# Attention with a 128-key window and a mixture of experts on one core: folding the two score blocks of a query block into one 128-wide tile, splitting the turned weights on GpSimd, and ordering TensorE's work by tiling

## The chip, the cores and the metric

The kernel runs on one core of a Trainium2 chip. The metric is device time in microseconds of one launch; before the change the median of three runs is 1196.53 us (1192.06 to 1199.35). Engines are named as in the profile: PE is TensorE (PEld its weight loads), DVE is VectorE, ACT is ScalarE, POOL is GpSimd, SP is SyncE.

## The reference

Shapes: 8 batches, 8 heads, 576 positions, 64 per head; then 4608 tokens of 512 features, 8 experts of 512 x 1024 x 512. All float32.

```python
scores = scale * np.matmul(q, k.transpose(0, 1, 3, 2))
rel = pos[:, None] - pos[None, :]
bias = slopes[:, None, None] * (-np.abs(rel))[None]
mask = (rel >= 0) & (rel < 128)
scores = np.where(mask, scores + bias[None], -1e9)
attn = softmax(scores); x = attn @ v            # then tokens x features
logits = x @ w_gate + log1p(exp(x @ w_noise)) * noise
# two largest experts of each token, softmax over the two
out[mask] += top2_w * (relu(x[mask] @ w1[e]) @ w2[e])
```

A query sees itself and the 127 keys before it: 128 keys in all. They lie in two neighbouring blocks of 128.

## The kernel before, in words

**Stages.** The attention runs over 32 head pairs (8 batches x 4). Five query blocks of a pair (four of 128 rows and a last one of 64, in which both heads share a tile) are taken in three units: blocks (0, 1), blocks (2, 3), block (4). A unit (L534) does the following.

- `scores` (L444; L454, and L447 for block 4): q times k for the block's own 128 keys and the 128 before them, so 256 columns (128 for block 0, 192 for block 4). Head 0 uses rows 0 to 63 of the array and writes bank 0, head 1 rows 64 to 127 and bank 1. There is only this one pair of score banks: the next unit's scores follow the reading of these.
- `top` (L466, L472, DVE): one instruction for each block and head adds the bias and the mask, writes `p` and keeps the extreme, over all 256 columns.
- `soft` (L475, L479, ACT): exp over the same columns, in place, with its sum.
- `trans` (L485, L491, PE): transposes `p` in pieces of 128 columns: two for each head of a block (one for block 0, two for block 4), so 6, 8 and 2 for the three units.
- `evac` (L494; copies are L244 on ACT, L248 on DVE): copies the turned weights from PSUM to `pT`, a copy for each block.
- `weigh` (L504, L522, PE): `pT` times the values, head 0 into columns 0 to 63 of the array and head 1 into columns 64 to 127. For block 4 two of the four products use the lower 64 rows only.

After four pairs the batch's result is normalized and turned to token rows (L631), its gate computed (L654, L665) and the routing done (L700 on): a chain of small DVE instructions that ends in a list of tokens for each expert, scattered by POOL (L842).

The first wave of the mixture computes 256 tokens of each of experts 0 to 3 in float32 (L1085, L1139); its products are strewn between the attention of the later batches and the start of the second wave. The second wave (from about 400 us on) takes all 8 experts in 20 blocks of 320 to 512 tokens, in float16 split into a high and a low part. A block has 8 steps. A step is a first product of 12 matmuls (`mm1` L1082, L1088: four chunks of three) into one bank; then ACT makes the high part (`relu`, L1110), DVE the low part from bank and high part (L1129), and the second product of 12 matmuls (L1143, or L1148 flipped) takes both. Three banks serve the first products in turn: 0, 1 (the former score banks) and 5.

**What sets the order.** A planner in the kernel (class `Order`) plays all strands of work forward with a cost and a rank for each piece and issues the instructions in the order it finds; the engines run that order as written. Constants such as `STAGE`, `LATE` and `FFN1` shift ranks. Where a buffer is used again, the tile framework adds the semaphore waits.

```python
bank = [psum.tile([128, 512], F32, name=f"bank{i}") for i in range(8)]
sb, tb, ob, yb = Ring([bank[0:2]]), Ring([*bank[2:4], bank[7]]), Ring([bank[4], bank[6]]), Ring([])
```

Of the kernel before, what the change touches and what calls it, by code (L numbers as in the profile page):

```python
# [37 lines left out]
ZERO = 8.2  # L38
LOAD = 43.5
VALUES = -12.4  # L40
GATE = (-41.8, -83.8)
ROUTE = 0
SCATTER = (10.0, -1028.0, -66.0)
FFN0, FFN1 = 100.4, 316.8
WEIGHTS = -48.4
TOKENS = 70.2
STAGE = (5.1, 1.9, 12.7, -7.9, -6.3, 14.0, -6.0, -21.8)
MIDDLE = 73.7
RESULT = -61.8
WEIGHTS_LATE = 82.3  # L50
SIZES = (40.0, 1000 - 52.0)
EARLY = 1
SOON = 49.9
TIGHT = (1, 5, 7)
LATE = (-2.2, 37.9, 22.2, 61.2, 4.9, 37.3, -6.2, -4.7, 1.9, 24.7, 19.5, 35.7)
LAG = 0.2
SP_COST = 0.55
# [18 lines left out]
class Op:  # L76


    def __init__(self, on, emit, join=True):
        self.on, self.emit, self.join, self.taken = on, emit, join, False  # L80
# [9 lines left out]
class Order:  # L90
# [3 lines left out]
    def __init__(self):  # L94
        self.heap, self.seq, self.now, self.dma = [], 0, 0.0, 0.0
        self.busy = {e: 0.0 for e in ("PE", "ACT", "DVE", "POOL", "SP")}
        self.queue = {e: [] for e in self.busy}
        self.alive = 0
        self.work = {}

# [49 lines left out]
    def dispatch(self, e):  # L150
        if self.busy[e] > self.now:
            return
        while self.queue[e]:
            _, _, us, what, strand = heapq.heappop(self.queue[e])
# [3 lines left out]
            what.emit(e) if len(what.on) > 1 else what.emit()  # L158
            end = self.products(us) if e == "PE" else self.now + us
# [6 lines left out]
            return  # L166

# [37 lines left out]
def attention_moe(ctx: ExitStack, tc: tile.TileContext, qk_, v, w_gate, w_noise, noise, w1, w2,  # L205
# [7 lines left out]
    bank = [psum.tile([128, 512], F32, name=f"bank{i}") for i in range(8)]  # L213
# [11 lines left out]
    def pe(us, rank, emit, join=True):  # L225
        return Op((("PE", us, rank),), emit, join)
# [30 lines left out]
    pr = ring(ap_, 3, [128, 2, 2, 256], F32, "p")  # L257
    nmr = ring(ap_, 3, [128, 2, 2], F32, "nm")
    ptr = ring(ap_, 3, [128, 2, 4, 128], F32, "pT")
# [17 lines left out]
    relc, m1 = scratch[0][:, 0:256], scratch[0][:, 256:512]  # L277
    relc4, m14 = scratch[1][:, 0:192], scratch[1][:, 192:384]
    ident = const.tile([128, 128], F32, name="ident")
    bias = const.tile([128, H, 256], F32, name="bias")  # L280
    bias4 = const.tile([128, NP, 192], F32, name="bias4")
# [28 lines left out]
    def slope(h):  # L310
        return -8.0 * 2.0 ** -(h + 1)

    def masks():
        def mask(rel, m):
            nc.vector.tensor_scalar(m, rel, 0.0, None, op0=OP.is_lt)
            nc.vector.scalar_tensor_tensor(m, rel, float(W), m, op0=OP.is_ge, op1=OP.add)
            nc.vector.scalar_tensor_tensor(rel, m, 2.0 ** 40, rel, op0=OP.mult, op1=OP.add)

        def bias_of(e, h):
            copy(e, bias[:, h, :], relc, scale=slope(h))  # L320
# [3 lines left out]
        yield dve(0.14, -40, lambda: nc.vector.tensor_scalar(ident, relc[:, 0:128], 128.0, None, op0=OP.is_equal))  # L324
        yield dve(0.14, -40, lambda: nc.vector.tensor_scalar(before, relc[:, 0:128], 128.0, None, op0=OP.is_lt))
        yield dve(1.1, -40, lambda: mask(relc, m1))
        yield dve(0.95, -40, lambda: mask(relc4, m14))
# [83 lines left out]
    def all_values():  # L411
        for y in range(2 * B):
# [3 lines left out]
            yield from move(5e5, rank - 3, lambda: nc.sync.dma_start(  # L416
                t[:, 0:4], dram(v, b * S * DM + c, [[DM, 128], [128 * DM, 4], [1, 256]])))
            yield from move(1.3e5, rank - 3, lambda: nc.sync.dma_start(
                t[:, 4], dram(v, (b * S + S - 128) * DM + c, [[DM, 128], [1, 256]])))
# [46 lines left out]
    def top(k, blocks, s, p, nm):  # L466
        g = k % NP
        for z, i in enumerate(blocks):
            c, o = width(i), place_of(blocks, z)
            for h in range(heads(i)):  # L470
                bv = bias4[:, g] if i == 4 else bias[:, 2 * g + h, 256 - c:256]
# [10 lines left out]
    def pieces(i):  # L482
        return 4 if 0 < i < 4 else 2
# [1004 lines left out]
```

## Time and profile before

| what | before |
|---|---|
| median of 3 runs | 1196.53 us (1192.06 to 1199.35) |
| span of the profiled execution | 1193.9 us, 2.6 us below that median |
| PE busy / instructions | 1146.1 us / 7164 |
| DVE, ACT, POOL busy | 712.7, 518.4, 223.9 us |
| attention's transposes (L491) | 512 |
| last scores of the attention start | 310 us |
| first product of the second wave | 402.6 us |

The span runs from the first to the last instruction of one execution; the time of a run also has what lies around it. In the groups of instructions a line reads: source line, engine, operation, output and inputs by the program's names, shape, count, then busy time and the mean of one in ns. Matmuls are pipelined, so the duration of one (379 ns for 512 columns) is longer than the distance to the next. The windows give the busy time of each engine in a stretch; the chain of waits follows the end of the program back from releaser to releaser; the timeline lists instructions by their start.

### The profile page before, as it was taken

How to read it: one execution, taken by the hardware profiler on the slowest of the kernel's cores; microseconds unless marked ns; L12 is line 12 of the kernel's file. 1: busy time of each engine (PE TensorE's matmuls, PEld its weight loads, DVE VectorE, ACT ScalarE, POOL GpSimd, SP SyncE). 2: the span in 40 equal slices, each digit the busy share in tenths (PEclk: the TensorE clock that was granted, in tenths of full speed). 3: DMA queues.
4: the chain of work that ended last, by engine and by line, in shares of the span. 5: the costliest groups of instructions: out<-in, count | busy, mean ns of one | idle time of the engine just before them, and what ended most of it. 6: DMA issues, size and time to landing. Idle time of an engine off the chain costs nothing.

```text
span 1193.9 us, 20221 instructions
## 1 busy us (share of the span) xinstructions
PE 1146.1 (96%) x7164; PEld 666.6 (56%) x7164; DVE 712.7 (60%) x2422; ACT 518.4 (43%) x1317; POOL 223.9 (19%) x280
## 2 busy tenths in 40 slices
PE   7999999999998999999999999999999999999995
PEld 5666666666665545545445445445645654575552
DVE  7898867787866846646646746733843573372310
ACT  7777766676423514424324334422523442262311
POOL 1000100010023113203303312322303320232211
PEclk9999999999999999999999999999999999999998
DMA  9897454553277736627618617632843481342221
GB/s 325 293 327 252 145 154 156 157 167 96 83 197 216 245 120 149 184 83 195 184 38 208 173 48 192 168 64 54 239 132 63 93 261 36 62 117 45 36 27 23
DMA packets 133623, 173.32 MB, mean 145 GB/s; under 512 B 25488, under 2 KB 85136, under 8 KB 133520
## 3 DMA queue, kind: packets, MB, share of 16 engines
q1 hardware_dynamic: 115600, 131.68, 34.7%
q0 software_dynamic: 17920, 40.33, 17.6%
q8 instruction: 57, 0.93, 0.3%
q14 instruction: 46, 0.38, 0.1%
HBM read 130.57 MB, written 41.40 MB: 144 GB/s over the span
## 4 chain that ended last, share of the span: by engine, by line
PE 79%; DVE 7%; DMA 7%; issue 4%; ACT 1%; POOL 1%; SPq 0%; POOLq 0%; another core or an unknown queue 0%; DVEq 0%; ACTq 0%
PE bank L1088 24%; PE bank L1143 17%; PE bank L1148 7%; PE bank L522 5%; PE bank L491 5%; DMA mraw<-in_w_dram 5%; PE bank L454 5%; PE bank L1085 4%; PE bank L1139 4%; PE bank L1068 2%; DVE wam L989 2%; PE bank L631 2%; PE bank L654 1%; DVE p L472 1%; PE bank L447 1%
## 5 line engine op out<-in xcount | busy, mean ns | idle before, releaser
L1129 DVE SCALAR_TENSOR_TENSOR bhl<-bank,bhh 128x512 f16<-128x512 f32 (+3 forms) x160 | 97.3, 608 | 302.0 <-ACT bhh L1110 295.7
L1110 ACT ACTIVATE bhh<-bank 128x512 f16<-128x512 f32 (+3 forms) x150 | 80.5, 537 | 361.5 <-PE bank L1088 358.1
L1088 PE MATMUL bank<-bxh,w1hb 128*128 128x512 f16 (+3 forms) x640 | 222.2, 347 | 0.0
L1088 PE MATMUL bank<-bxl,w1hb 128*128 128x512 f16 (+3 forms) x640 | 222.1, 347 | 0.0
L1088 PE MATMUL bank<-bxh,w1lb 128*128 128x512 f16 (+3 forms) x640 | 222.1, 347 | 0.0
L1222 POOL DMA_INDIRECT out_dram<-yo,ix x72 | 113.2, 1572 | 562.4 <-ACT yo L244 484.7
L1088 PEld LDWEIGHTS <-w1hb 128*128 128x128 f16 x1280 | 124.4, 98 | 106.1 <-issue 2.2
L1143 PE MATMUL bank<-w2hb,bhl 128*128 128x512 f16 (+1 forms) x376 | 142.6, 379 | 6.9 <-DVE bhl L1129 6.9
L1143 PE MATMUL bank<-w2hb,bhh 128*128 128x512 f16 (+1 forms) x376 | 142.8, 380 | 0.5 <-ACT bhh L1110 0.5
L1143 PE MATMUL bank<-w2lb,bhh 128*128 128x512 f16 (+1 forms) x376 | 142.5, 379 | 0.0
L479 ACT ACTIVATE p<-p,nm 128x256 f32<-128x256 f32 (+2 forms) x288 | 133.7, 469 | 10.7 <-DVE nm L472 10.6
L1143 PEld LDWEIGHTS <-bhh 128*128 128x128 f16 (+1 forms) x752 | 72.0, 98 | 78.5 <-issue 4.6
L472 DVE CUSTOM_DVE_ANT_0 p<-bank,bias 128x256 f32<-128x256 f32 (+2 forms) x288 | 95.7, 382 | 25.4 <-PE bank L454 21.9
L1088 PEld LDWEIGHTS <-w1lb 128*128 128x128 f16 x640 | 62.6, 98 | 55.0
L522 PE MATMUL bank<-pT,vraw 128*64 128x128 f32 (+3 forms) x896 | 81.2, 303 | 2.4 <-ACT pT L244 1.4
L491 PE MATMUL bank<-ident,p 128*128 128x128 f32 x512 | 80.9, 284 | 1.3 <-ACT pT L244 0.5
L989 DVE TENSOR_REDUCE wam<-mraw 128x1 f32<-128x1024 f32 x56 | 67.7, 1211 | 22.2 <-DMA mraw<-in_w_dram 21.6
L1036 POOL DMA_INDIRECT xg<-xs_dram,ix x72 | 70.7, 981 | 44.3 <-issue 18.5
L454 PE MATMUL bank<-qk 64*128 64x256 f32 (+1 forms) x512 | 68.3, 383 | 8.6 <-DMA qk<-in_qk_dram 4.7
L522 PEld LDWEIGHTS bank<-pT,vraw 128*64 128x64 f32 (+1 forms) x896 | 51.2, 136 | 41.6 <-issue 7.7
L1148 PE MATMUL bank<-bhl,w2hb 128*128 128x448 f16 (+1 forms) x224 | 73.8, 330 | 0.0
L1148 PE MATMUL bank<-bhh,w2hb 128*128 128x448 f16 (+1 forms) x224 | 73.8, 330 | 0.0
(201 smaller groups left out, 1716.6 us busy)
## 6 DMA issues: line engine op xcount, KB each, us to landing
raw<-in_w_dram SPq DMA_DIRECT2D x128, 256.0 KB
mraw<-in_w_dram SPq DMA_DIRECT2D x56, 512.0 KB
qk<-in_qk_dram SPq DMA_DIRECT2D x32, 608.0 KB
out_dram<-xg SPq DMA_DIRECT2D x10, 1024.0 KB
vraw<-in_v_dram SPq DMA_DIRECT2D x16, 512.0 KB
w1a<-in_w_dram SPq DMA_DIRECT2D x32, 256.0 KB
w2a<-in_w_dram SPq DMA_DIRECT2D x32, 256.0 KB
xs_dram<-x SPq DMA_DIRECT2D x32, 256.0 KB
```

The lines of the kernel that those rows point to most:

```text
L454: nc.tensor.matmul(s[h][:, o:o + c], qk[half, i * 128:i * 128 + 128], qk[half, QW + k0:QW + k0 + c], start=True, stop=True)
L472: nc.vector.tensor_tensor_reduce(out=p[:, z, h, 0:c], in0=s[h][:, o:o + c], in1=bv, scale=-0.125, scalar=3.0e38, op0=OP.add, op1=OP.min, a ...
L479: nc.scalar.activation(pv, pv, AF.Exp, bias=nm[:, z, h:h + 1], scale=-1.0, accum_out=den[:, z, 2 * g + h:2 * g + h + 1])
L491: nc.tensor.transpose(t[:, z], p[:, h, a:a + 128], ident)
L522: nc.tensor.matmul(o[half, o0:o0 + c], t[p0:128, kb, hh:hh + D], w, start=m == 0, stop=m == len(lst) - 1)
L989: yield dve(1.13, rank, lambda: nc.vector.tensor_reduce(o, t, axis=AX.X, op=OP.max, apply_absolute_value=True))
L1088: nc.tensor.matmul(t[:, 0:blk.n], wp[:, c], x[:, c, 0:blk.n], start=c == 0 and z == 0, stop=c == 3 and z == 2)
L1110: nc.scalar.activation(o, i, AF.Relu)
L1129: yield dve(0.07 + c * 0.00104, rank - MIDDLE, lambda: nc.vector.scalar_tensor_tensor(hl[:, 0:c], t[:, 0:c], 0.0, hh[:, 0:c], op0=OP.max, ...
L1143: nc.tensor.matmul(blk.y[j][0:r], h[:, cs], wp, start=f == 0 and m == 0, stop=f == 7 and m == 2)
L1148: nc.tensor.matmul(blk.y[c][:, 0:blk.n], wp[:, c * 128:c * 128 + 128], h[:, 0:blk.n], start=f == 0 and m == 0, stop=f == 7 and m == 2)
L1222: ins = nc.gpsimd.indirect_dma_start(out=out, out_offset=bass.IndirectOffsetOnAxis(ap=blk.ix[0:r, j:j + 1], axis=0), in_=t[0:r], in_offset ...
```

## The change

**Softmax over 128 keys.** The two score banks become one tile `pair` of two banks. Before `top`, a new DVE instruction (`copy_predicated`) overwrites, in the older block's 128 columns, those keys that lie in the query's own block (key not after query) with the scores of the own block: what remains are just the 128 keys the query sees. `top`, `soft`, `p`, the bias and `trans` then run over 128 columns: 4, 4 and 1 transposes for a unit, into one bank, with one `evac`. The rings for `p`, the extremes and `pT` have 4 buffers (3 before).

**Split on GpSimd.** The turned tile holds own and older keys mixed. Two `affine_select` instructions for each unit write the own part to a second place and zero the rest, then zero the own keys in the first. `weigh` stays as it was, but for block 4 both products use all 128 rows; the values come with the last 128 keys as a fifth block, in one DMA instead of two.

**Order.** The planner knows a tiling for each piece of PE work, charges 0.093 for a change of it, and prefers a piece of the present tiling if its rank is within 1.8 of the first. Its constants were set anew.

```diff
-STAGE = (5.1, 1.9, 12.7, -7.9, -6.3, 14.0, -6.0, -21.8)
+STAGE = (-27.0, 0.6, 1.1, -7.9, -6.3, 1.2, -6.0, -21.8)
+SWITCH, NEAR = 0.093, 1.8
+TOP, SOFT, SPLIT = (1.28, 1.55, 0.45), (1.56, 1.56, 0.4), (0.8, 1.34, 0.54)
...
+            at = self.like() if e == "PE" else 0
...
+            if e == "PE" and what.mode != self.mode:
+                us, self.mode = us + SWITCH, what.mode
...
+    def like(self):
+        q = self.queue["PE"]
+        near = [(x[:2], z) for z, x in enumerate(q) if x[3].mode == self.mode and x[0] <= q[0][0] + NEAR]
+        return min(near)[1] if near else 0
...
-    bank = [psum.tile([128, 512], F32, name=f"bank{i}") for i in range(8)]
+    pair = psum.tile([128, 2, 512], F32, name="pair")
+    bank = [pair[:, 0], pair[:, 1], *(psum.tile([128, 512], F32, name=f"bank{i}") for i in range(2, 8))]
...
-    pr = ring(ap_, 3, [128, 2, 2, 256], F32, "p")
+    pr = ring(ap_, 4, [128, 2, 2, W], F32, "p")
...
     def top(k, blocks, s, p, nm):
+        if blocks == (4,):
+            nc.vector.copy_predicated(s[0][:, 0:64], own_key4.bitcast(U32), s[0][:, W:W + 64])
+        else:
+            z0 = blocks[0] == 0
+            sv = pair[:, :, 128 * z0:512 - 128 * z0].rearrange("p h (z a c) -> p h z a c", a=2, c=W)
+            shape = [128, 2, 2 - z0, W]
+            nc.vector.copy_predicated(sv[:, :, :, 0], own_key.bitcast(U32)[:, None, None, :].to_broadcast(shape), sv[:, :, :, 1])
...
+    def trans(blocks, p, t):
+        for z, i in enumerate(blocks):
+            for h in range(heads(i)):
+                c = (2 * h + z) * W
+                nc.tensor.transpose(t[:, c:c + W], p[:, z, h], ident)
...
+    def split(blocks, pt):
...
+        nc.gpsimd.affine_select(b, a, pattern, OP.is_ge, nothing, base=0, channel_multiplier=-1)
+        nc.gpsimd.affine_select(a, a, [[-x, c] for x, c in pattern], OP.is_gt, nothing, base=0, channel_multiplier=1)
...
+        yield pool(SPLIT[gr], r5, lambda: split(blocks, pt))
```

Over the whole program the order has 288 attention transposes (512), 96 `copy_predicated`, 192 `affine_select`, 96 copies of turned weights on ACT or DVE, 64 of 512 columns and 32 of 128 (160 before, 96 of 512 and 64 of 256), and 277 changes of PE's tiling (305). The names below end in buffer numbers; `[waits X_49]` is a wait for engine X's semaphore.

PE in the attention before the change, a stretch of the second batch: scores are L454 and L447, transposes L491, weighted values L522.

```order
L454 MATMUL bank_66<-qk_78 128x256 [waits DVE_49]
L454 MATMUL bank_67<-qk_78 128x256 [waits DVE_49]
L454 MATMUL bank_66<-qk_78 128x256
L454 MATMUL bank_67<-qk_78 128x256
L522 MATMUL bank_72<-pT_92,vraw_83 64x256 [waits DVE_49]
L522 MATMUL bank_72<-pT_92,vraw_83 64x256
L522 MATMUL bank_72<-pT_92,vraw_83 64x128 x4
L491 MATMUL bank_73<-ident,p_85 128x128 [waits DVE_49,Activation_49]
L491 MATMUL bank_73<-ident,p_85 128x128 [waits Activation_49]
L522 MATMUL bank_70<-pT_93,vraw_83 64x64 x4
```

The same kind of stretch of PE in the changed program (scores L483 and L476, transposes L523, weighted values L564).

```order
L483 MATMUL pair<-qk_79 128x256 [waits DVE_49]
L483 MATMUL pair<-qk_79 128x256 x3
L564 MATMUL bank_69<-pT_92,vraw_83 64x256 [waits Pool_49]
L564 MATMUL bank_69<-pT_92,vraw_83 64x256
L564 MATMUL bank_69<-pT_92,vraw_83 64x128 x4
L564 MATMUL bank_71<-pT_93,vraw_83 64x64 [waits DVE_49,Activation_49,Pool_49]
L564 MATMUL bank_71<-pT_93,vraw_83 64x64 x3
L523 MATMUL bank_72<-ident,p_86 128x128 [waits DVE_49,Activation_49]
L523 MATMUL bank_72<-ident,p_86 128x128 [waits Activation_49] x3
L476 MATMUL pair<-qk_79 128x192 [waits DVE_49]
```

Pieces of the same tiling now stand together (both L564 pieces), a unit has 4 transposes or 1, the weighted values wait for POOL instead of the copying engine, and the next scores stand four transposes after two pieces of weighted values.

PE in the second wave before the change, where the first product of one step (into bank 1) follows that of the step before (bank 0) without anything between: L1088, `w1hb3`/`w1hb4` being the weights of the two steps.

```order
L1088 MATMUL bank0_66<-bxl0_4005,w1hb3_4025 128x512
L1088 LDWEIGHTS w1lb3_4026
L1088 MATMUL bank0_66<-bxh0_4003,w1lb3_4026 128x512
L1088 LDWEIGHTS w1hb4_4029
L1088 MATMUL bank1_67<-bxh0_4003,w1hb4_4029 128x512
L1088 LDWEIGHTS w1hb4_4029
L1088 MATMUL bank1_67<-bxl0_4005,w1hb4_4029 128x512
L1088 LDWEIGHTS w1lb4_4030
L1088 MATMUL bank1_67<-bxh0_4003,w1lb4_4030 128x512
L1088 LDWEIGHTS w1hb4_4029
L1088 MATMUL bank1_67<-bxh0_4003,w1hb4_4029 128x512
```

The same place in the changed program (L1121; the step of `w1hb6` writes the second half of `pair`, the step before it wrote the first half).

```order
L1121 MATMUL pair_66<-bxh0_3977,w1hb6_4011 128x512
L1121 LDWEIGHTS w1hb6_4011
L1121 MATMUL pair_66<-bxl0_3979,w1hb6_4011 128x512
L1121 LDWEIGHTS w1lb6_4012
L1121 MATMUL pair_66<-bxh0_3977,w1lb6_4012 128x512
L1121 LDWEIGHTS w1hb6_4011
L1121 MATMUL pair_66<-bxh0_3977,w1hb6_4011 128x512 [waits Activation_49]
L1121 LDWEIGHTS w1hb6_4011
L1121 MATMUL pair_66<-bxl0_3979,w1hb6_4011 128x512
L1121 LDWEIGHTS w1lb6_4012
L1121 MATMUL pair_66<-bxh0_3977,w1lb6_4012 128x512
L1121 LDWEIGHTS w1hb6_4011
```

The matmuls stand in the same order, but the second chunk of three now waits for ACT, and the third chunk, whose first row follows next, for DVE. Over the second wave's first products (1920 matmuls) one waits for ACT and none for DVE before the change; in the changed program 43 wait for ACT and 58 for DVE, all on `pair`.

More of the change, by code (lines that the diff above doesn't have):

```diff
@@ L153, in dispatch @@
         while self.queue[e]:
-            _, _, us, what, strand = heapq.heappop(self.queue[e])
+            at = self.like() if e == "PE" else 0
+            _, _, us, what, strand = self.queue[e][at]
+            if at:
+                self.queue[e][at] = self.queue[e][-1]
+                self.queue[e].pop()
+                heapq.heapify(self.queue[e])
+            else:
+                heapq.heappop(self.queue[e])
             if what.taken:
@@ L313, in masks, with window, full, halves @@
     def masks():
[L314 to L317, printed above, removed]
+        def window(out_, rel_):
+            nc.vector.tensor_scalar(out_, rel_, 0.0, float(W), op0=OP.is_lt, op1=OP.mult)
+            nc.vector.tensor_add(out_, out_, rel_)
+        def full():
+            nc.vector.tensor_scalar(own_key, rel, 0.0, None, op0=OP.is_ge)
+            window(rel2[:, 0], rel)
+            nc.vector.tensor_scalar(rel2[:, 1], rel, 0.0, 2.0 ** 40, op0=OP.is_lt, op1=OP.mult)
+            nc.vector.tensor_add(rel2[:, 1], rel2[:, 1], rel)
+        def halves():
+            nc.vector.tensor_scalar(own_key4, rel4[:, 0:64], 0.0, None, op0=OP.is_ge)
+            window(relc4, rel4)
         def bias_of(e, h):
-            copy(e, bias[:, h, :], relc, scale=slope(h))
+            copy(e, bias[:, :, h], rel2, scale=slope(h))
             part = slice(h % 2 * 64, h % 2 * 64 + 64)
             copy(e, bias4[part, h // 2], relc4[part], scale=slope(h))
[L324 to L327, printed above, removed]
+        yield dve(0.14, -40, lambda: nc.vector.tensor_scalar(ident, rel, 0.0, None, op0=OP.is_equal))
+        yield dve(0.14, -40, lambda: nc.vector.tensor_scalar(before, rel, 0.0, None, op0=OP.is_lt))
+        yield dve(1.0, -40, full)
+        yield dve(0.6, -40, halves)
         for g in range(NP):
@@ L517, in weigh @@
                 if blocks == (4,):
-                    w, c = pt[p0:128, 0, at, half], D
+                    w, c = pt[:, 0, at, half], D
                 else:
@@ L521, in weigh @@
                     w = pt.rearrange("p h s c -> p h (s c)")[:, h, at * 128:at * 128 + c]
-                nc.tensor.matmul(o[half, o0:o0 + c], t[p0:128, kb, hh:hh + D], w, start=m == 0, stop=m == len(lst) - 1)
+                nc.tensor.matmul(o[half, o0:o0 + c], t[:, kb, hh:hh + D], w, start=m == 0, stop=m == len(lst) - 1)
     over, attended = Event(n + B), Event(n)
@@ L543, in unit @@
         s = yield (sb, r0)
-        yield pe((0.95, 1.2, 0.36)[gr], r0, lambda: scores(k, blocks, s))
+        yield pe((0.95, 1.2, 0.36)[gr], r0, lambda: scores(k, blocks, s), mode="rows" if nz == 2 else "full")
         left[k] -= 1
@@ L549, in unit @@
         nm = yield (nmr, r1)
[L550 removed]
+        yield dve(TOP[gr], r1, lambda: top(k, blocks, s, p, nm))
         put(sb, s)
@@ L583, in unit @@
         mark(over)
-    def part(blocks, z, a, pt, r4, parted):
-        i = blocks[z]
-        yield either((0.27, 0.48, 0.48, 0.48, 0.27)[i], (0.34, 0.6, 0.6, 0.6, 0.34)[i], r4, LATE[3],
-                     lambda e: evac(e, blocks, z, a, pt))
-        put(tb, a)
-        mark(parted)
     def rows(b, gr, t):
@@ L1466 @@
         qk[:, h, :, 512 + 64 * h:512 + 64 * h + 64] = q[:, h, :, 512:]
+    values = a["v"].transpose(0, 2, 1, 3).reshape(B, S, DM)
     arrays = {
         "in_qk_dram": qk,
-        "in_v_dram": a["v"].transpose(0, 2, 1, 3).reshape(N, DM),
+        "in_v_dram": _np.concatenate([values, values[:, S - 128:S - 64]], axis=1),
         "in_w_gate_dram": a["moe_w_gate"],
```

123 lines of the change are left out of this document (59 added, 64 removed).

## The prediction

> **What bounds the kernel now.** I read the page first, then busy time by stretch, then groups by shape, then the timeline at the places that the change touches.
>
> ```profile
> span 1193.9 us, 20221 instructions
> PE 1146.1 (96%) x7164; PEld 666.6 (56%) x7164; DVE 712.7 (60%) x2422; ACT 518.4 (43%) x1317; POOL 223.9 (19%) x280
> PE 79%; DVE 7%; DMA 7%; issue 4%; ACT 1%; POOL 1%; SPq 0%; POOLq 0%; another core or an unknown queue 0%; DVEq 0%; ACTq 0%
> ```
>
> PE is busy for 96% of the span and holds 79% of the chain of waits: what is taken from PE comes off the end, and what PE waits comes on top. The busy share hides waits (durations overlap), so it has to be seen by stretch.
>
> ```profile
> core 0: us, PE busy (x) PEld busy (x) DVE busy (x) ACT busy (x) POOL busy (x), PEclk, DMA share, GB/s
> 0.00:50.00 50.00, 41.90 (x341) 28.65 (x342) 39.63 (x167) 39.51 (x138) 3.18 (x24) 1.00 0.92 308
> 100.00:150.00 50.00, 45.34 (x431) 32.31 (x428) 42.22 (x226) 37.03 (x140) 5.37 (x6) 1.00 0.57 185
> 300.00:350.00 50.00, 50.00 (x373) 33.36 (x372) 39.48 (x183) 19.12 (x63) 6.75 (x8) 1.00 0.48 132
> 450.00:1180.00 730.00, 716.67 (x3912) 384.98 (x3911) 375.51 (x922) 256.41 (x439) 172.16 (x199) 1.00 0.47 117
> ```
>
> In the first 150 us, before the first wave's products fill PE, DVE is at 80 to 84% and PE has gaps of 5 to 8 us in 50: there two engines are near their end. Later PE is full; in the second wave it is idle for 13 us of 730, while DVE and ACT have half their time free. A microsecond of new PE waiting in the second wave is therefore a microsecond of the end, and there are 730 us in which to collect them.
>
> **What leaves PE.** The price of a transpose is the distance between starts, not its duration.
>
> ```profile
> 288.26 1.04 PE L491 MATMUL bank<-ident,p 128*128 128x128 f32 x8
> 289.13 1.03 PE L1085 MATMUL bank<-axh,w1a 128*128 128x256 f32 x4
> 290.00 0.60 PE L491 MATMUL bank<-ident,p 128*128 128x128 f32 x4
> 290.53 0.87 PE L522 MATMUL bank<-pT,vraw 128*64 128x256 f32 x8
> ```
>
> Eight transposes take 289.13 - 288.26 = 0.87 us, 0.109 each, when work of the same tiling (128\*128) follows. Four of them ahead of column-tiled work (128\*64) take 0.53 where 4 x 0.109 = 0.44: the change of tiling costs 0.09. The order goes from 512 to 288 transposes: 224 x 0.109 = **-24.4 us**. Tiling changes fall from 305 to 277: 28 x 0.093 = **-2.6 us**. The values' DMA (one for two) runs ahead of its use and counts nothing; were it late, 16 issues of SP are all that it could save or cost.
>
> **What goes to DVE, ACT and POOL in the attention.**
>
> ```profile
> L472 DVE CUSTOM_DVE_ANT_0 p<-bank,bias 128x256 f32<-128x256 f32 x192 | 71.0, 420 | 11.1 <-PE bank L454 10.2 <-PE bank L491 0.5
> L472 DVE CUSTOM_DVE_ANT_0 p<-bank,bias 128x128 f32<-128x128 f32 x64 | 15.9, 286 | 12.2 <-PE bank L454 11.7 <-PE bank L491 0.5
> L248 DVE COPY pT<-bank 128x512 f32<-128x512 f32 x26 | 17.9, 687 | 5.0 <-PE bank L491 3.6 <-ACT pT L244 0.8 <-ACT p L479 0.4
> L248 DVE COPY pT<-bank 128x256 f32<-128x256 f32 x28 | 11.8, 421 | 6.3 <-ACT xu L244 2.6 <-PE bank L491 2.4 <-PE bank L522 1.3
> L248 DVE COPY xul<-bank 128x64 f32<-128x64 f32 x14 | 3.0, 217 | 2.2 <-PE bank L522 1.8
> L472 DVE CUSTOM_DVE_ANT_0 p<-bank,bias 128x192 f32<-128x192 f32 x32 | 11.2, 349 | 2.1 <-PE bank L447 1.9
> L479 ACT ACTIVATE p<-p,nm 128x256 f32<-128x256 f32 x192 | 94.7, 497 | 1.9 <-DVE nm L472 1.9
> L479 ACT ACTIVATE p<-p,nm 128x128 f32<-128x128 f32 x64 | 24.9, 395 | 3.5 <-DVE nm L472 3.5
> L365 POOL MEMSET xg<- 128x512 f32 x1 | 0.5, 534 | 0.0
> ```
>
> For a head pair, `top` was 2 x 0.286 + 6 x 0.420 + 0.349 = 3.44 us and becomes 9 x 0.286 = 2.57, plus the three predicated copies. Those are not in the trace; the nearest rows are copies out of PSUM of the same sizes, 0.687 + 0.421 + 0.217 = 1.33. Bounds: half of that, if two columns went at once, and twice, if reading and rewriting the bank took a pass each; I take the rows. So +0.46 a pair, 15 us of DVE over 32 pairs. The order gives DVE 17 turned-weight copies of 512 columns and 7 of 128 where it had 26 of 512 and 28 of 256: -16 us. DVE stays even. ACT loses 192 x 0.10 us of exp and some 20 us of copies and gains room; it is not what PE waits for.
>
> A select on POOL is not in the trace either: the memset of 512 columns writes without reading, 0.53 us, and is the lower bound; twice that (a pass to read, a pass to write), 1.07, the upper. At 0.7, and 0.42 and 0.28 for 256 and 128 columns, six of them make 2.8 us a pair, of some 10 us at which pairs follow (32 in 310 us). POOL is nearly empty there (3 to 7 us in 50), so throughput is no matter; a select now lies between copy and weighted values, 0.6 to 1.4 us later than before, for which the order leaves two to three us of other PE work in most units, less in some.
>
> What does matter is the one pair of score banks.
>
> ```profile
> PEld bank L454 <- DVE nm L472: 6.9, 11, 1.8
> PE bank L454 <- DVE nm L472: 3.7, 5, 1.1
> ```
>
> PE already waits for `top` before scores. Its work between two scores shrinks by seven transposes, 0.76 us a pair, while `top` gets longer, so part of what is saved is waited away, most of all in the first half, where DVE is at 84%. Of the 27 us some 13 fall into the first half; I take half of these as waited away (7) and 5 us for late selects: **+12 us**. Bounds: -3 (ACT's room removes waits of its own) and +27 (nothing is gained).
>
> **What the two-bank tile costs later.** After the attention the score banks serve the second wave's first products, as two of three banks. Before, they were two tiles; now they are one, and the order's waits show what follows. The place before the change, with 448 columns:
>
> ```profile
> 470.20 0.35 PE L1088 MATMUL bank<-bxh,w1lb 128*128 128x448 f16 x1
> 470.39 0.35 PE L1088 MATMUL bank<-bxh,w1hb 128*128 128x448 f16 x1
> 470.65 0.54 ACT L1110 ACTIVATE bhh<-bank 128x448 f16<-128x448 f32 x1 [1.08 <-PE bank L1088]
> 470.76 0.35 PE L1088 MATMUL bank<-bxh,w1lb 128*128 128x448 f16 x1
> 470.95 0.35 PE L1088 MATMUL bank<-bxh,w1hb 128*128 128x448 f16 x1
> 471.22 0.62 DVE L1129 SCALAR_TENSOR_TENSOR bhl<-bank,bhh 128x448 f16<-128x448 f32 x1 [0.65 <-ACT bhh L1110]
> 471.52 0.35 PE L1088 MATMUL bank<-bxh,w1hb 128*128 128x448 f16 x1
> ...
> 417.49 0.68 DVE L1129 SCALAR_TENSOR_TENSOR bhl<-bank,bhh 128x512 f16<-128x512 f32 x1
> 418.23 0.39 PE L1143 MATMUL bank<-w2hb,bhl 128*128 128x512 f16 x1 [2.54 <-DVE bhl L1129]
> ```
>
> The step's last matmul starts at 470.20; the next step begins at 470.39 in the other bank, its second chunk at 470.95, its third at 471.52; meanwhile ACT (from 470.65, 0.45 after the last matmul's start) and DVE read the first bank. Nothing holds PE. In the changed program the second chunk waits for ACT's reading and the third for DVE's. And these readers wait too: the count of PE's semaphore that ACT waits for is, in 46 of 160 steps, that of the third matmul of the next step, since that was recorded ahead of the reader as a write into the same tile. So they take turns. Chunk one ends with the matmul at 470.76; ACT starts 0.45 later, 471.21, ends 471.75; PE goes on 0.06 later (the last two rows: 417.49 + 0.68 = 418.17, then 418.23), at 471.81 and not 470.95: 0.86 lost. The chunk's third matmul starts 0.37 later, 472.18; DVE from 472.63 to 473.25; PE at 473.31 and not 0.57 after 471.81, 472.38: 0.93 lost. **1.8 us for one handover.** At 512 columns, where half of them are, it is 1.87 (ACT 0.60, DVE 0.69); at 320 some 1.5.
>
> ```profile
> L1110 ACT ACTIVATE bhh<-bank 128x512 f16<-128x512 f32 x64 | 38.2, 597 | 181.4 <-PE bank L1088 178.1 <-issue 2.4
> L1129 DVE SCALAR_TENSOR_TENSOR bhl<-bank,bhh 128x512 f16<-128x512 f32 x64 | 44.0, 688 | 137.6 <-ACT bhh L1110 137.5
> L1110 ACT ACTIVATE ahh<-bank 128x256 f32<-128x256 f32 x13 | 5.0, 384 | 15.3 <-PE bank L1085 14.0 <-issue 1.2
> ```
>
> 42 handovers carry both waits: 42 x 1.76 = **+74 us**. Lower bound 37, if only one of the two readings holds PE; upper 95, if ACT or DVE are at other work when it is their turn (their queues hold the scaling of weights, 0.7 us apiece). Six first-wave products wait for ACT in the same way, 0.38 + 0.28 us each: **+4**. A slower PE gives those that feed it time, so of PE's present 13 us of idleness and the small waits under them I let **8** go. The second wave starts earlier by what the attention gains: 62 us of first-wave products stand behind the last attention matmul (54 before), which cover the last batch's routing.
>
> Sum: -24.4 - 2.6 + 12 + 74 + 4 - 8 = **+55 us**. Span 1193.9 + 55 = 1249; on the median, 2.6 above the span, 1251. I say **1250**.
>
> **The rivals.**
>
> *The handovers cost nothing, and the change is faster (0.11).* If the waits are met before PE arrives (readers quicker than I take them, or PE not held by a wait within a chunk group), what is left is -27 + 12 = -15 to -20: 1178. For it: PE holds the order unchanged and ACT idles 178 us for L1088. Against: the reader is released only by the very chunk behind which PE stops. It decides below 0.4 us a handover, where 42 of them no longer outweigh 15 us.
>
> *Half is absorbed (0.14).* PE's queue of the second wave may have waited under its overlapping durations for more than 13 us, or the handover costs one reading: 1196.5 - 15 + 37 - 5 = 1213. Half of this lies within 1%.
>
> *DVE becomes the bound of the attention (0.07).* At twice the copy's price the predicated copies add 43 us to a DVE at 80 to 84%; then nothing of the 27 is kept: 1277.
>
> *GpSimd becomes the bound (0.03).* From 1.6 us for a mean select (six in 10 us, three times my price) each pair takes what its selects take. At ten times the memset for 512 columns, 5.3, and in proportion, 18.6 us a pair: 32 x 18.6 = 595 us for an attention of 310, about 1530. [...]
>
> **How the numbers follow.** The forecast has 0.65, rivals 0.11, 0.14, 0.07 and 0.03. Against no change, of which a measurement can tell about 1%: faster 0.11, within 1% 0.07 (half of the second rival), slower 0.82. The forecast alone spans 1222 (handovers at 1.1 us) to 1282 (their upper bound and the attention's). The range reaches to the half-absorbed case and the doubled copies: 1200 to 1288, which leaves out the faster case, the slow selects and some tails.
>
> **What would show it.** Right: 288 transposes at 0.109; last scores at about 290 to 300 us; the second wave's first product at 385 to 395; from there to the end about 65 us longer than before; PE waits in the groups of the first product, released by ACT's and DVE's readings, some 0.85 and 0.9 us each, about 40 times each; selects of 0.5 to 1.1 us for 512 columns. Wrong: a second wave no longer than before (handovers free), or an attention that does not end earlier than 310 us (loop, DVE or POOL).

## The result, and the profile after

| what | before | after |
|---|---|---|
| median | 1195.8 us (1192.1 to 1199.4) | 1265.5 us (1264.6 to 1266.3) |
| ratio, 95% interval | | 1.058 (1.054 to 1.061) |
| span of the profiled execution | 1193.9 us | 1264.6 us |
| last weighted values of the attention start | 323.1 us | 298.6 us |
| first product of the second wave starts | 402.8 us | 399.3 us |
| from there to the end | 791.1 us | 865.3 us |

The change makes the kernel 70 us slower; 1250 was forecast, in a range of 1200 to 1288. (Before the change the second wave's first product starts at 402.8 us; at 402.6 the last first product of the first wave starts.) The page of the changed kernel, its two lines of totals and its chain of waits:

```profile
span 1264.6 us, 20114 instructions
PE 1137.7 (90%) x6940; PEld 644.2 (51%) x6940; DVE 715.9 (57%) x2473; ACT 483.2 (38%) x1300; POOL 310.5 (25%) x472
PE 69%; DVE 12%; DMA 8%; issue 6%; ACT 2%; POOL 1%; SPq 1%; DVEq 0%; another core or an unknown queue 0%; POOLq 0%; ACTq 0%
```

PE is busy for 8 us less and stands for 69% of the chain, not 79: its time goes into waiting. PE's busy time in three stages (attention, rest of the first wave, second wave), cut at the table's starts. Columns: stretch, its length, PE busy with the number of instructions, granted clock, DMA share, GB/s. First the kernel before, then the changed one.

```profile
0.00:323.10 323.10, 308.39 (x2655) 1.00 0.61 196
323.10:402.80 79.70, 76.69 (x397) 1.00 0.75 212
402.80:1193.90 791.10, 760.98 (x4118) 0.99 0.47 118
```

```profile
0.00:298.60 298.60, 269.76 (x2369) 0.99 0.65 207
298.60:399.30 100.70, 91.36 (x460) 0.95 0.67 188
399.30:1264.60 865.30, 776.58 (x4118) 0.99 0.43 107
```

The attention ends 24.5 us earlier, 21 of which are gone before the second wave starts; the second wave has the same 4118 instructions and takes 74.2 us longer. What PE waited for most in the changed kernel (total, times, longest):

```profile
PE pair L1121 <- DVE bhl L1162: 31.1, 40, 1.7
PE pair L1121 <- ACT bhh L1143: 25.4, 39, 0.7
PE pair L483 <- DVE nm L509: 12.2, 15, 1.6
PE pair L1118 <- ACT ahh L1143: 9.3, 6, 6.9
PE pair L1121 <- DVE fit L468: 7.4, 5, 3.2
```

Every one is for the tile `pair`. Before the change the second wave's first product had no such wait in the list. One handover from the timeline, at 448 columns like the one that the prediction was worked from:

```profile
472.59 0.35 PE L1121 MATMUL pair<-bxh,w1lb 128*128 128x448 f16 x1
473.04 0.55 ACT L1143 ACTIVATE bhh<-pair 128x448 f16<-128x448 f32 x1 [1.65 <-PE pair L1121]
473.63 0.35 PE L1121 MATMUL pair<-bxh,w1hb 128*128 128x448 f16 x1 [0.69 <-ACT bhh L1143]
473.82 0.35 PE L1121 MATMUL pair<-bxl,w1hb 128*128 128x448 f16 x1
474.01 0.35 PE L1121 MATMUL pair<-bxh,w1lb 128*128 128x448 f16 x1
474.48 0.62 DVE L1162 SCALAR_TENSOR_TENSOR bhl<-pair,bhh 128x448 f16<-128x448 f32 x1 [2.08 <-PE pair L1121]
475.15 0.35 PE L1121 MATMUL pair<-bxh,w1hb 128*128 128x448 f16 x1 [0.79 <-DVE bhl L1162]
```

PE, ACT, PE, DVE, PE take turns. Matmuls of this shape follow one another in 0.19 us, so PE would have gone on at 472.78 and 474.20; it went on at 473.63 and 475.15: 0.85 and 0.95 lost, 1.80 together. What the profile names as idle is less, 0.69 and 0.79, because a matmul's duration (0.35) reaches beyond the start of its follower (0.19 on).

The five waits named for `fit`, a value of one column, are handovers too. The profile puts a wait down to what came last, and in all five DVE's reading of `pair` stands straight in front of `fit`. The longest:

```profile
1027.93 1.22 DVE L1022 TENSOR_REDUCE wam<-mraw 128x1 f32<-128x1024 f32 x1 [3.42 <-DMA mraw<-in_w_dram]
1029.07 0.68 DVE L1162 SCALAR_TENSOR_TENSOR bhl<-pair,bhh 128x512 f16<-128x512 f32 x1
1029.67 0.14 DVE L468 TENSOR_SCALAR fit<-fit 128x1 int32<-128x1 int32 x1
1029.81 0.59 PE L1121 MATMUL pair<-bxh,w1hb 128*128 128x512 f16 x1 [3.21 <-DVE fit L468]
```

DVE's reading (L1162) stood in its queue behind a maximum over weights whose DMA came late; it ended at 1029.75, and PE went on 0.06 later.

The instructions that the trace of before could not show:

```profile
L543 POOL TENSOR_SCALAR_AFFINE_SELECT pT<-pT 128x512 f32<-128x512 f32 x32 | 21.6, 675 | 76.2 <-ACT pT L263 60.3 <-PE bank L687 9.5 <-DVE pT L267 3.7
L504 DVE COPY_PREDICATED pair<-own_key,pair 128x512 f32<-128x512 uint32 x32 | 22.1, 691 | 9.1 <-PE pair L483 8.9
```

A select of 512 columns takes 0.68 us (0.7 assumed), a choice of 512 columns 0.69, as the copy out of PSUM of that size in the kernel before (0.687).

### The profile page after: what moved, and what is told of

The parts are those of the page before. It is cut to its first block, busy times and chain, and to the rows that moved or that the text cites. A ratio compares the mean times of both kernels' runs of the same rounds, so it can differ in the third digit from the quotient of the medians.

```text
span 1264.6 us, 20114 instructions
## 1 busy us (share of the span) xinstructions
PE 1137.7 (90%) x6940; PEld 644.2 (51%) x6940; DVE 715.9 (57%) x2473; ACT 483.2 (38%) x1300; POOL 310.5 (25%) x472
## 4 chain that ended last, share of the span: by engine, by line
PE 69%; DVE 12%; DMA 8%; issue 6%; ACT 2%; POOL 1%; SPq 1%; DVEq 0%; another core or an unknown queue 0%; POOLq 0%; ACTq 0%
PE bank L1176 17%; PE pair L1121 16%; PE bank L1121 8%; PE bank L1181 7%; DMA mraw<-in_w_dram 4%; PE bank L1172 3%; PE bank L564 3%; PE pair L483 3%; DVE bhl L1162 2%; PE bank L1101 2%; PE bank L1118 2%; PE bank L523 2%; DVE wam L1022 2%; PE pair L1118 2%; DVE p L509 2%
## 5 line engine op out<-in xcount | busy, mean ns | idle before, releaser
L1121 PEld LDWEIGHTS <-w1hb 128*128 128x128 f16 x1280 | 124.0, 98 | 187.8 <-issue 91.6
L1162 DVE SCALAR_TENSOR_TENSOR bhl<-pair,bhh 128x512 f16<-128x512 f32 (+3 forms) x107 | 64.8, 606 | 262.9 <-PE pair L1121 133.9
L1121 PE MATMUL pair<-bxh,w1hb 128*128 128x512 f16 (+3 forms) x428 | 148.1, 346 | 67.5 <-DVE bhl L1162 31.1
L1121 PE MATMUL pair<-bxh,w1lb 128*128 128x512 f16 (+3 forms) x428 | 148.3, 347 | 0.0
L1121 PE MATMUL pair<-bxl,w1hb 128*128 128x512 f16 (+3 forms) x428 | 148.2, 346 | 0.0
L516 ACT ACTIVATE p<-p,nm 128x128 f32<-128x128 f32 x288 | 111.8, 391 | 16.8 <-DVE nm L509 16.0
L1121 PEld LDWEIGHTS <-w1lb 128*128 128x128 f16 x640 | 62.6, 98 | 55.6 <-issue 0.8
L1162 DVE SCALAR_TENSOR_TENSOR bhl<-bank,bhh 128x512 f16<-128x512 f32 (+3 forms) x53 | 32.6, 615 | 99.9 <-ACT bhh L1143 99.9
L483 PE MATMUL pair<-qk 64*128 64x256 f32 (+1 forms) x512 | 69.3, 391 | 17.3 <-DVE nm L509 12.2
L564 PE MATMUL bank<-pT,vraw 128*64 128x128 f32 (+2 forms) x896 | 76.7, 302 | 1.9 <-POOL pT L544 1.6
L1121 PE MATMUL bank<-bxh,w1hb 128*128 128x512 f16 (+3 forms) x212 | 74.5, 351 | 0.0
L1121 PE MATMUL bank<-bxl,w1hb 128*128 128x512 f16 (+3 forms) x212 | 74.4, 351 | 0.0
L1121 PE MATMUL bank<-bxh,w1lb 128*128 128x512 f16 (+3 forms) x212 | 74.4, 351 | 0.0
```

Source lines behind the costliest of these rows:

```text
L483: nc.tensor.matmul(s[h][:, o:o + c], qk[half, i * 128:i * 128 + 128], qk[half, QW + k0:QW + k0 + c], start=True, stop=True)
L516: nc.scalar.activation(pv, pv, AF.Exp, bias=nm[:, z, h:h + 1], scale=-1.0, accum_out=den[:, z, 2 * g + h:2 * g + h + 1])
L564: nc.tensor.matmul(o[half, o0:o0 + c], t[:, kb, hh:hh + D], w, start=m == 0, stop=m == len(lst) - 1)
L1121: nc.tensor.matmul(t[:, 0:blk.n], wp[:, c], x[:, c, 0:blk.n], start=c == 0 and z == 0, stop=c == 3 and z == 2)
L1162: yield dve(0.07 + c * 0.00104, rank - MIDDLE, lambda: nc.vector.scalar_tensor_tensor(hl[:, 0:c], t[:, 0:c], 0.0, hh[:, 0:c], op0=OP.max, ...
```

## Experiments

The first question is whether the shared tile causes the loss, or something else that the change did to the order or to the engines. Two kernels answer it from both sides: one takes the tile away and keeps the rest of the change, one brings nothing but the tile.

**The change with two tiles.** The order of instructions on PE, ACT and POOL is that of the changed kernel; DVE has a second choice in 64 units.

```diff
-    pair = psum.tile([128, 2, 512], F32, name="pair")
-    bank = [pair[:, 0], pair[:, 1], *(psum.tile([128, 512], F32, name=f"bank{i}") for i in range(2, 8))]
+    bank = [psum.tile([128, 512], F32, name=f"bank{i}") for i in range(8)]
...
-            nc.vector.copy_predicated(sv[:, :, :, 0], own_key.bitcast(U32)[:, None, None, :].to_broadcast(shape), sv[:, :, :, 1])
+            for x in s:
+                sv = x[:, 128 * z0:512 - 128 * z0].rearrange("p (z a c) -> p z a c", a=2, c=W)
+                nc.vector.copy_predicated(sv[:, :, 0], own_key.bitcast(U32)[:, None, :].to_broadcast(shape), sv[:, :, 1])
```

> The changed kernel with the folded tile taken apart again: the two score banks are two tiles, as before, and the choice between the two halves of the scores (copy_predicated) is issued once for each bank, 64 instructions more on VectorE. Every other instruction, and its order on TensorE, VectorE, ScalarE and GpSimd, is that of the changed kernel. Theory A (the two halves share one tile, so that a product into one half waits for the readers of the other): the second wave takes 791 us again and not 865, the 43 ScalarE and 39 to 43 VectorE waits on the tile are gone from it; the wait of 9.3 us in the first wave's products after the attention goes too, so the second wave starts at 386 to 392 and not at 399; in all 1180 us (1172 to 1190). Theory B (the waits stand for something else that the change did, such as later ReLUs or an engine that became slower): they stay under another tile's name, 1250 us or more. Theory C (the waits covered others, which come out when they go): 1205 to 1235 us.

Measured: 1187.2 us (1181.2 to 1192.9), ratio to the kernel before 0.993 (0.991 to 0.995). Its three stages:

```profile
0.00:296.80 296.80, 274.62 (x2369) 0.99 0.66 209
296.80:392.10 95.30, 90.00 (x461) 0.96 0.72 202
392.10:1184.50 792.40, 763.07 (x4118) 0.99 0.48 116
```

Theory A. The second wave is back at 792.4 us, and its first product is no longer among PE's waits. The start of the second wave, 392.1, lies at the late end of what was expected. Against the changed kernel the stages are 1.8, 5.4 and 72.9 us shorter.

**The kernel before with nothing but the tile.** The first of the two edits above, reversed, in the kernel before.

> The kernel before with one edit: its two score banks are the halves of one tile. No instruction is added, removed or moved on any engine. Theory A (sharing a tile is the cost): the second wave takes 865 us and not 791, with some 40 waits for ScalarE and 40 for VectorE; with a few us more in the first wave 1270 us (1255 to 1290). Theory B (something else in the change is the cost): within 10 us of the kernel before, 1186 to 1206 us. Theory C (half of it): 1225 to 1245 us.

Measured: 1267.2 us (1262.6 to 1268.5), ratio 1.059 (1.056 to 1.062). Its last two stages, and its waits:

```profile
325.00:409.50 84.50, 79.00 (x396) 0.98 0.73 205
409.50:1265.40 855.90, 775.08 (x4118) 0.99 0.44 108
```

```profile
PE pair L1089 <- DVE bhl L1130: 33.0, 40, 1.9
PE pair L1089 <- ACT bhh L1111: 21.1, 33, 1.0
```

Theory A again: one line that adds and moves no instruction costs 72 us, 65 of them in the second wave (855.9 against 791.1, nine short of the 865 expected), 5 in the stage before it and 2 in the attention, which ends at 325.0. With the experiment above this is shown from both sides. What it costs is no property of the banks: in the kernel before, with two tiles, the prediction's timeline has ACT (from 470.65) and DVE (from 471.22) read one bank while PE writes the next, from 470.39 on in steps of 0.19, and with two tiles in the changed kernel the second wave runs at its old pace, 792.4 us against 791.1. The one tile makes the readings of one bank hold the writes to the other, and the 72.9 us of the second wave are the price of that here.

**One half left idle.** If only the neighbourhood of the two halves does harm, taking a bank away should help.

```diff
-        for t in sb.free.pop():
-            put(hbr, t)
+        put(hbr, sb.free.pop()[0])
```

> The changed kernel, but after the attention only one half of the shared tile goes to the FFN's products; the other lies idle, so that they have two banks instead of three. Theory A (the halves harm each other only where products stand in both, and two banks carry the ring, as ScalarE and VectorE give a bank back within 2 us and a step takes 5): the waits for the other half are gone, 1182 to 1205 us, although a bank is taken away. Theory B (the third bank is needed): new waits for ReLU and remainder on the two banks, 1215 to 1260 us.

Measured: 1194.8 us (1191.7 to 1197.2), ratio 0.999 (0.998 to 1.001). Theory A: with two banks for the first products instead of three the kernel is 71 us faster than with three of which two share a tile.

**One tile in the attention, two afterwards.** The tile is given up after the last scores, and two tiles take its two banks.

```diff
+    scoring = ExitStack()
-    pair = psum.tile([128, 2, 512], F32, name="pair")
+    pair = scoring.enter_context(tc.tile_pool(name="scoring", bufs=1, space=PSUM)).tile([128, 2, 512], F32, name="pair")
...
-        for t in sb.free.pop():
-            put(hbr, t)
+        sb.free.pop()
+        scoring.close()
+        halves = main.enter_context(tc.tile_pool(name="halves", bufs=1, space=PSUM))
+        for z in range(2):
+            put(hbr, halves.tile([128, 512], F32, name=f"half{z}"))
```

> The changed kernel as it is through the attention, with one tile for both score banks and one choice a unit; after the attention that tile is given up, and two tiles of one bank each take its place for the products of the FFN. The order on TensorE, VectorE, ScalarE and GpSimd is that of the changed kernel. Theory A (the cost is the shared tile in the FFN, and in the attention the choice in one piece is worth 0.155 us of VectorE a unit): 2 to 5 us faster than the kernel with two tiles throughout, 1182 to 1186 us. Theory B (the attention gains as much from two tiles as it loses by two choices): within 2 us of it, 1185 to 1189 us. Theory C (giving up the tile makes the first products in the new ones wait): over 5 us slower than it.

Measured: 1192.4 us (1187.4 to 1198.8), ratio 0.997 (0.995 to 0.999). No theory had this quite: the second wave is in order (794.2 us), so nothing waits for the tile that was given up, yet it is 5 us slower than with two tiles throughout (the intervals of the two ratios touch, at 0.995). In the two profiles 4 us of it are lost in the attention, whose last weighted values start at 301.0 and not 296.8. The changed kernel (298.6) and the one with an idle half (302.6) have the same attention, so single profiles of it lie 4 us apart: that two choices beat one, though they are busy longer, is likely and not shown. The experiment bank by bank, below, gives a reason for it.

With the tile out of the way the second question comes up: the two-tile kernel has 27 us less for PE to do, and is 8 us faster. Where are the other 19?

**Without the choice.** The choice is left out, so part of the scores is not read.

```diff
-            for x in s:
-                sv = x[:, 128 * z0:512 - 128 * z0].rearrange("p (z a c) -> p z a c", a=2, c=W)
-                nc.vector.copy_predicated(sv[:, :, 0], own_key.bitcast(U32)[:, None, :].to_broadcast(shape), sv[:, :, 1])
```

> As the one with two tiles, but the choice between the two halves of the scores is left out (no copy_predicated at all), so that only the first half of each pair of scores is read. It takes 0.69 us for a unit of two 512-wide tiles, or 0.42, out of the loop in which the next unit's scores wait for VectorE. Theory A (the score loop is bound by VectorE, and TensorE's 33 us of waits there are real): the attention ends 10 to 20 us earlier than with the choice, and the whole is 8 to 16 us shorter. Theory B (the scores wait anyway for something else, or TensorE's other work fills the time): within 3 us of the kernel with two tiles.

Measured: 1180.4 us (1179.7 to 1180.8), ratio 0.987 (0.986 to 0.989): 7 us below the two-tile kernel, the attention's last weighted values at 288.2 instead of 296.8. Nearer to theory A, with both figures just short of its bounds. DVE's part of the loop of scores is felt, but 47 us less of DVE (40.0 for the units of two blocks, 7.1 for the last blocks; by durations, which overlap: DVE's busy time falls by 37) buy only 9 us of attention.

**Bank by bank.** Choice and maxima of the first head's bank, then those of the second's.

```diff
+            for h, x in enumerate(s):
+                sv = x[:, 128 * z0:512 - 128 * z0].rearrange("p (z a c) -> p z a c", a=2, c=W)
+                nc.vector.copy_predicated(sv[:, :, 0], own_key.bitcast(U32)[:, None, :].to_broadcast(shape), sv[:, :, 1])
+                for z, i in enumerate(blocks):
+                    best(g, i, z, h, s, p, nm, blocks)
```

> As the kernel with two tiles, but VectorE takes the choice and the maxima bank by bank: choice and maxima of the first head's bank, then those of the second's; before, both choices came first and the maxima alternated. No instruction is added. The first bank is then free after half of VectorE's work and not after three of four maxima. Theory A (the next unit's scores wait for the first bank): their wait for VectorE of 8.2 us in 11 products and 17.1 us in 28 weight loads shrinks by a third or more, 2 to 6 us shorter in all. Theory B (TensorE takes its products in turn, and the second one waits for the second bank anyway): within 2 us of the kernel with two tiles.

Measured: 1198.7 us (1194.2 to 1200.5), ratio 1.001 (1.000 to 1.003): 11 us slower than the two-tile kernel, which neither theory had; the attention ends at 306.6. DVE's timeline gives a reason. One unit of 512 columns in the two-tile kernel (x2 is two instructions in a row):

```profile
180.09 0.76 DVE L504 COPY_PREDICATED bank<-own_key,bank 128x256 f32<-128x256 uint32 x2
180.75 0.28 DVE L509 CUSTOM_DVE_ANT_0 p<-bank,bias 128x128 f32<-128x128 f32 x1
...
181.60 0.69 DVE L667 TENSOR_TENSOR x<-bank,den 128x512 f32<-128x512 f32 x1
```

And the same kind of unit, bank by bank:

```profile
187.31 0.43 DVE L504 COPY_PREDICATED bank<-own_key,bank 128x256 f32<-128x256 uint32 x1
187.77 0.29 DVE L513 CUSTOM_DVE_ANT_0 p<-bank,bias 128x128 f32<-128x128 f32 x1
...
188.20 0.42 DVE L504 COPY_PREDICATED bank<-own_key,bank 128x256 f32<-128x256 uint32 x1
188.66 0.29 DVE L513 CUSTOM_DVE_ANT_0 p<-bank,bias 128x128 f32<-128x128 f32 x1
...
189.09 0.69 DVE L671 TENSOR_TENSOR x<-bank,den 128x512 f32<-128x512 f32 x1
```

In the first, two choices and the step to the first maximum take 180.75 - 180.09 = 0.66, 0.33 for each: what follows a choice reads the other bank and starts before the choice, 0.42 long, is over. In the second every choice is followed by the maximum that reads what it wrote, and that starts 0.46 later, after its end. The unit takes 189.09 - 187.31 = 1.78 instead of 1.51: 0.13 more for each of 128 choices (at 128 columns 0.20 and 0.33, so 0.13 again), 17 us in all; the attention ends 10 us later. Whether it is the same output or only the same bank that holds the follower, these runs do not tell apart. The choice in one piece has the same fault once a unit: the first maximum always reads what was just written. In the changed kernel it starts 0.73 after a choice of 0.70, and a unit of 512 columns takes 1.58 (from its choice at 181.38 to what follows its maxima at 182.96), though it has one instruction less; that this is all of the 5 us between one choice and two was not tried.

**With one of the two selects.** Leaves out a part of the weights' split.

```diff
-        nc.gpsimd.affine_select(a, a, [[-x, c] for x, c in pattern], OP.is_gt, nothing, base=0, channel_multiplier=1)
```

> As the kernel with two tiles, but the second of GpSimd's two selects of each unit is left out, so that one half of the turned weights keeps what belongs to the other. TensorE, VectorE and ScalarE have the same instructions in the same order. With two tiles TensorE waited for the second select 9.8 us in 22 weight loads and 2.4 us in 4 products, and a select takes 0.65, 0.41 or 0.29 us. Theory A (the selects are late and this sets the end of the attention): the attention ends 4 to 9 us earlier, the whole is 3 to 8 us shorter. Theory B (the weighted values would wait for something else, or other work fills the time): within 2 us of the kernel with two tiles.

Measured: 1185.9 us (1181.1 to 1188.3), ratio 0.991 (0.989 to 0.993). The attention ends 4.1 us earlier, as theory A had it, but the whole is 1.4 us shorter, less than the measurement resolves. Late selects cost the end little, if anything.

**Turned weights by ACT alone.** A repair that takes 13.7 us of copies off DVE and leaves nothing out.

```diff
-        yield either(*((0.48, 0.6) if nz == 2 else (0.17, 0.2)), r4, LATE[3], lambda e: evac(e, blocks, a, pt))
+        yield act(0.48 if nz == 2 else 0.17, r4, lambda: evac("ACT", blocks, a, pt))
```

> As the kernel with two tiles, but the turned weights are always copied out of their bank by ScalarE; with two tiles, 24 of these copies were on VectorE (13.7 us, 0.57 us each) and 72 on ScalarE. Nothing is left out; the planner places the rest anew. Theory A (VectorE's time in the attention is what TensorE waits for): the attention ends 3 to 7 us earlier, the whole is 2 to 6 us shorter. Theory B (the copies on ScalarE, which is two thirds busy with the exponentials, come later than VectorE would have made them): 2 to 10 us longer.

Measured: 1183.7 us (1179.8 to 1189.3), ratio 0.991 (0.989 to 0.993); the attention ends at 292.7. That leans to theory A, but its interval overlaps that of the two-tile kernel. Against the kernel before, both are faster, by under 1%.

**Without the tiling rule.** PE's next piece goes by rank alone.

```diff
-        return min(near)[1] if near else 0
+        return 0
```

> As the one with two tiles, but TensorE's next work is chosen by rank alone, without the preference for work in the same tiling. Theory A (a change of tiling costs 0.093 us, and the rule saves some tens of them): 2 to 4 us longer than with the rule. Theory B (the order that the rule makes matters more than the changes of tiling, because other work is moved with it): up to 10 us either way. Theory C: no difference, within 1 us.

Measured: 1192.5 us (1190.8 to 1196.7), ratio 0.998 (0.997 to 1.000): 5 us slower than with the rule. The rule is worth more than the 2.6 us that were put down for its tilings. In the two profiles the second wave starts at 392.1, and the rest of the difference lies behind it, where the rule's own subject, the attention, is over; so it looks like theory B's kind of effect, with the plan's other moves carrying it; no run took that apart.

**The plan at other costs.** The planner counts DVE's unit at 1.6, 1.85 and 0.55 us.

```diff
-TOP, SOFT, SPLIT = (1.28, 1.55, 0.45), (1.56, 1.56, 0.4), (0.8, 1.34, 0.54)
+TOP, SOFT, SPLIT = (1.6, 1.85, 0.55), (1.56, 1.56, 0.4), (0.8, 1.34, 0.54)
```

> As the kernel with two tiles, but the planner counts VectorE's choice and maxima of a unit at what the trace shows for two choices (1.6, 1.85 and 0.55 us, not 1.28, 1.55 and 0.45). No instruction is added; the order is planned anew. Theory A (the plan puts scores too early behind a VectorE that is slower than planned, and TensorE's waits there are the plan's): the score waits fall by a third, 3 to 8 us shorter. Theory B (the loop itself is what takes the time, whatever the plan): within 3 us either way. Theory C (the other numbers of the plan were chosen with these costs, and fit worse now): 3 to 10 us longer.

Measured: 1197.5 us (1194.3 to 1199.9), ratio 1.002 (1.001 to 1.003): theory C, 10 us slower. The expectation's premise was wrong: it had added up durations, where starts count. The unit above takes 1.51 us, and the plan's 1.55 was right.

## Why the prediction was right, and where it was not

**Handovers, +74: right in mechanism, some 8 us short in size.** Nothing but the tile costs 72 us in the kernel before, and its removal from the changed kernel gives 72.9 us of second wave. That is what was left after some of it had been absorbed. PE's waits on `pair` in the second wave of the changed kernel come to 67.6 us in 88 waits; in the handover above each was named 0.16 too short, and with 0.16 more for each they make an estimated 82 us. The single handover was priced right: 0.85 and 0.95 were lost where 0.86 and 0.93 had been worked out. On top came four waits more than the 84 of 42 handovers, and two late readings, of 1.9 and 3.2 us, with DVE at other work when its turn came, which the prediction had only as an upper bound. Of the two rivals, "handovers cost nothing" is refuted by the kernel before with the tile, "half is absorbed" by the same number.

**Absorbed, -8: right.** PE's waits in the second wave for anything but `pair` come to 16.2 us with two tiles and to 7.9 in the changed kernel; in the kernel before they are 17.4, and 10.9 with the tile. The one that shrank most, with two tiles and in the changed kernel (issue stands for idle time for which the profile shows no releaser):

```profile
PE bank L1101 <- issue: 7.3, 4, 2.1
PE bank L1101 <- issue: 2.1, 1, 2.1
```

82 less 8 is 74, against the 72.9 measured. Handovers and absorption together were to make 66 us of second wave, so what falls 7 short is the handovers.

**First-wave handovers, +4: right in sum by luck, wrong in kind.** The stage is 5.4 us shorter with two tiles. But the six waits are not 0.66 each: one is 6.9, the other five come to 2.4. Around it, in the changed kernel:

```profile
366.97 1.03 PE L1118 MATMUL pair<-axh,w1a 128*128 128x256 f32 x4
367.84 1.88 PE L1172 MATMUL bank<-w2a,ahh 128*128 128x512 f32 x4
369.55 0.60 PE L1101 MATMUL bank<-ident,xg 128*128 128x128 f32 x4
...
374.61 0.72 ACT L263 ACTIVATE xg<-xg,fit 128x512 f32<-128x512 f32 x1 [0.80 <-DVE fit L469]
377.69 0.72 ACT L263 ACTIVATE w1hb<-raw,wsc 128x512 f16<-128x512 f32 x1 [2.36 <-DMA raw<-in_w_dram]
378.32 0.36 ACT L1143 ACTIVATE ahh<-pair 128x256 f32<-128x256 f32 x1
378.74 1.22 PE L1118 MATMUL pair<-axh,w1a 128*128 128x256 f32 x2 [6.85 <-ACT ahh L1143]
```

ACT's reading of `pair` stood in its queue behind a scaling of tokens and a scaling of weights whose DMA had not landed; PE stood behind the reading. With two tiles there is one wait of 5.3 us left at this place, of a second product for the same kind of reading; so the queue is late whatever the tile is.

**Transposes and tilings, -27, and attention waits, +12: the first right, the second too small.** The 288 transposes follow one another in 0.109 us at the median, as before. The attention with two tiles ends 26.3 us earlier than before. But only 8.1 us arrive at the end, so the waits that the fold brings are -8.1 + 27 = 19, between the 12 put down and the upper bound of 27. The step that failed is the one that let the second wave start earlier "by what the attention gains", at 385 to 395: it started at 399.3, and at 392.1 with two tiles. The prediction had seen the 62 us of first-wave products behind the last attention matmul, 54 before, and took them as cover; they are work that had filled PE's gaps in the longer attention and now came after it. The groups of the stage, of the kernel before and of the two-tile kernel:

```profile
L1085 PE MATMUL bank<-axh,w1a 128*128 128x256 f32 x152 | 37.3, 382 | 0.0
L1139 PE MATMUL bank<-w2a,ahh 128*128 128x512 f32 x72 | 35.0, 600 | 2.5 <-issue 2.5
```

```profile
L1118 PE MATMUL bank<-axh,w1a 128*128 128x256 f32 x174 | 43.4, 385 | 0.0
L1172 PE MATMUL bank<-w2a,ahh 128*128 128x512 f32 x84 | 42.5, 623 | 5.3 <-ACT ahh L1143 5.3
```

22 and 12 more. By the starts quoted above, 0.87 us for four and 1.71 for four, that is 4.8 + 5.1 = 10 of the 15.6 us by which this stage grew (79.7 to 95.3); the longer wait makes 3, and the rest goes with a lower granted clock (0.96 in the stage, 1.00 before), for which no run here shows a cause. The 10 us are work that moved, not work that was added: taken off the 26.3, they leave 16 of the 27 gained in the attention. So of the 18 us lost by the spans (27 less 9.4), an estimated 11 are lost in the attention, 6 in the stage behind it and 1 in the second wave.

In the attention itself the prices of choice and select were right; it is DVE's loop that was under-rated. Without the choice its end comes 8.6 us earlier, and 7 of the 19 us come back; with 17 us more of it 11 more are lost; the late selects, 5 us in the prediction, are not seen at the end. What makes up the other 12 was not settled by a run. The plan's fit is one candidate, since a plan with a wrong cost for DVE loses 10. The granted clock is another: its mean is 0.985 to 0.993 in the nine executions of the two-tile kernel and 0.993 to 0.997 in those of the kernel before beside them, and among the nine the fastest has the highest (1181.2 us, 0.993), the slowest the lowest (1192.9, 0.985). The medians, 0.989 and 0.995, are 0.006 apart; of 1128 us of busy PE that is an estimated 7 us, part of which is in the 11 and the 6 already; that the clock is the cause, and not a result of PE's gaps, is not shown.

**The rival that made DVE the bound** had the right engine and the wrong size: DVE holds the loop of scores, but at the copy's price, not twice. Its 1277 does not follow from its own terms: with nothing of the 27 kept they give 1196.5 + 74 + 4 - 8 = 1266.5, within 1 us of what was measured. That is chance, since 8 us of the 27 were kept and the handovers cost more. (In the same way the forecast's upper end, 1282, comes to 1250 + 21 + 15 = 1286.) **GpSimd as the bound** is out: a select of 512 columns took 0.68 us, where this rival had 5.3. Its ten times the memset was the author's assumption, which no run shows; the runs show 1.3 times (0.68 against 0.53).

Sum of what was measured: -27 + 19 in the attention and the first wave, + 1.8 + 5.4 + 72.9 for the tile = 72, against 70 in the medians and 71 in the spans. The forecast's 55 lacks 7 for the attention's waits, 7 for the handovers of the second wave and 3 for the tile in the stages before it (1.8 + 5.4 against 4).

## What to carry to other kernels

Before two buffers are made one tile to save an instruction, follow each of them to its last use: the dependency was kept for the whole tile, and here it cost 73 us in a stage that has nothing to do with the instruction it was made for. A stage that gets shorter can give back work that had filled its gaps, 10 us here; take that work off the gain seen at the stage's end. On VectorE it paid to put something else between a choice and the instruction that reads its output: the kernel with two choices in a row was 11 us faster than the one bank by bank.

## What the runs showed of the hardware

- After a choice of 256 columns on VectorE, an instruction that read what it wrote started 0.46 us after its start, one that read another bank 0.33 us: 0.13 us for each such pair.
- A choice (copy_predicated, in PSUM) took 0.69, 0.42 and 0.22 us for 512, 256 and 64 columns, and so did a copy out of PSUM (0.687, 0.421 and 0.217 in the kernel before). The first GpSimd select of a unit took 0.68, 0.43 and 0.31 us for 512, 256 and 128, the second 0.65, 0.41 and 0.30.
- Two banks served this ring of products almost as well as three (1194.8 against 1192.4 us with the same attention; second waves of 800.7 and 794.2 us), so that a third bank with a wrong dependency (1265.5 us) was worse than none.
